# The sums of layer two's weight blocks as single steps, each tied behind VectorE's newest eviction or maximum

## The chip, the cores and the metric

The kernel runs on one core of a Trainium2 chip. The metric is the device time in microseconds (us) of one execution. Three runs of the kernel before gave 817.4, 818.07 and 819.8 us; their median is 818.07 us. TensorE multiplies matrices into PSUM, VectorE and ScalarE work elementwise and read PSUM, GpSimd works elementwise in SBUF, and SyncE issues the transfers.

## The reference, cut to what matters

Attention whose keys are masked by a hash bucket, then two feed-forward layers. Layer one squares a rectified product; layer two (`moe2`) has a leaky activation.

```python
mask = q_bucket[:, :, :, None] == k_bucket[:, :, None, :]
scores = np.where(mask, scale * np.matmul(q, k.transpose(0, 1, 3, 2)), -1000000000.0)
attn = np.exp(scores - np.max(scores, axis=-1, keepdims=True))
attn = attn / (np.sum(attn, axis=-1, keepdims=True) + 1e-09)
x = heads_side_by_side(np.matmul(attn, v))        # 1536 tokens x 512
h = np.maximum(x @ w_in, 0.0)                      # 512 x 2048
x = h * h @ w_out                                  # 2048 x 512
h = x @ w_in2
out = (np.maximum(h, 0.0) + alpha * np.minimum(h, 0.0)) @ w_out2
```

The host hands the layers' weights over as the bits of float64; the kernel turns them into float32 itself.

## The kernel before, in words

The tokens are cut into four chunks of 384. Attention for chunk 0 comes first. Then layer one runs chunk by chunk (`feed_forward`, 16 steps over the hidden blocks `f`), and while chunks 0 to 2 go through it, the attention of chunks 1 to 3 is issued in between (`following`), in steps that `beside` calls five times per hidden block. A second list of steps, `conversion`, is issued in the same way from the start of chunk 1 to progress 2.9 (chunk 2 nearly done). Layer two comes after all that; its input products use sums of weight blocks (a scheme with seven products for eight), so its weights must be ready in DRAM by then, as float32 and with the sums.

One step of attention of concern here: `scores` multiplies on TensorE (L386), VectorE takes the negated maximum of 128x768 scores (L391, `low`), ScalarE the exponential (L394, `sm`). `p_t` transposes the exponentials on TensorE (L409), and the 128x384 result is copied out of PSUM either by ScalarE (L413) or by VectorE (L415), as a letter in `EVICT` says. These copies are called evictions here. `k_ids` makes a mask (L277) and `hash_bits` a comparison (L241) on VectorE.

The conversion of one weight block (`to_f32`): SyncE loads 512 KB into one of three buffers of the pool `wide` (L603), ScalarE makes the exponent (L613), VectorE masks the sign (L615), shifts the mantissa in (L616) and joins the two (L621); the scratch tiles have one buffer each. For a block of `w_out2` the result goes to DRAM (`ahead`, L628). For `w_in2`, blocks `f` and `f + 8` are a pair (`sums_ahead`): their converted halves a11, a12 and a21, a22 stay in the first half of their `wide` buffers, four sums of 128x256 are written into the second halves by VectorE (L649 to L652), and two stores take the seven parts to DRAM (L654, L655). There are 8 pairs. A pair has eight steps before: load and convert the first block; load and convert the second block, with the four sums and both stores; then load and convert of two blocks of `w_out2`, in turn. All 64 steps are spread evenly over 1.9 chunks.

The order on each engine's queue is the planner's. It goes through the program in the order of issue, and lets an instruction that it takes to be ready go before an earlier one that it takes to be waiting. `tc.add_manual_dep(later, earlier, NoSync)` is an order that the planner must keep; between two instructions of one engine it needs no semaphore. Layer one's own weights are fetched by SyncE (L683, `wf`), split by ScalarE (L665) and VectorE or GpSimd (L666), in the same stretch.

Of the kernel before, what the change touches and what calls it, by code (L numbers as in the profile page):

```python
# [7 lines left out]
F32 = mybir.dt.float32  # L8
# [5 lines left out]
ALU = mybir.AluOpType  # L14
# [15 lines left out]
def kernel(  # L30
# [20 lines left out]
    nc = tc.nc  # L51
# [3 lines left out]
    P = 128  # L55
# [11 lines left out]
    def pool(name, bufs, stack=ctx, **kw):  # L67
        return stack.enter_context(tc.tile_pool(name=name, bufs=bufs, **kw))

    const = pool("const", 1)  # L70
    dram = pool("scr", 1, space=DRAM)
# [10 lines left out]
    state = {"attention": True, "moe": False, "s": 0, "m": 0, "h": 0, "whole": state_whole}  # L82
# [14 lines left out]
    def s_tile():  # L97

        state["s"] += 1
        if not state["moe"] and state["s"] % 2 == 0:  # L100
            return ps_a.tile([P, 3, 512], F32, tag="acc", name="acc")
        return ps_s.tile([P, 2, 512], F32, tag="s", name="s")

    def m_tile():

        state["m"] += 1
        if not state["moe"] and state["m"] % 3 == 0:
            return ps_h.tile([P, 512], F32, tag="h", name="h")
        return ps_m.tile([P, 512], F32, tag="m", name="m")
# [94 lines left out]
    class Pair:  # L204
# [175 lines left out]
        def scores(self, h, t):  # L380
            ps = s_tile()
            qs = slice(t * P, (t + 1) * P)
            for a in range(2):
                ks = slice(a * HALF, (a + 1) * HALF)
                for i in range(2):
                    nc.tensor.matmul(  # L386
                        ps[:, a, 0:HALF], self.q[:, h, i, qs], self.k[:, h, i, ks], start=i == 0, stop=i == 1
                    )

            low = p4.tile([P, 1], F32, tag="low", name="low")  # L390
            low_ins = nc.vector.tensor_reduce(low, ps[:, 0:2, 0:HALF], AX.XY, ALU.max, negate=True)  # L391
            sm = sm3.tile([P, S], F32, tag="sm", name="sm")
            i = h * NTB + t
            sm_ins = nc.scalar.activation(  # L394
                sm.rearrange("p (a n) -> p a n", a=2), ps[:, 0:2, 0:HALF], AF.Exp, bias=low,
                accum_out=self.sums[:, i:i + 1],
            )
            scored[self.c, self.j, i] = (low_ins, sm_ins)
            self.p[h, t] = sm

        def p_t(self, h, t, a):
            if t == 0 and a == 0:
                self.pt[h] = p2.tile([P, NTB, NKB, P], F32, tag="pt", name="pt")
            pp = self.p[h, t]
            ps = m_tile()
            n = NKB // 2
            for i in range(n):
                b = a * n + i
                nc.tensor.transpose(ps[:, i * P:(i + 1) * P], pp[:, b * P:(b + 1) * P], ident)  # L409
            src = ps[:, 0:n * P].rearrange("p (b n) -> p b n", b=n)  # L410
            dst = self.pt[h][:, t, a * n:(a + 1) * n, :]
            if EVICT[self.c][2 * t + a] == "a":
                nc.scalar.activation(dst, src, AF.Copy)  # L413
            else:
                nc.vector.tensor_copy(dst, src)  # L415

        def av(self, part):

# [175 lines left out]
    w_bits = {}  # L594
# [5 lines left out]
    def load_bits(u):  # L600
        l, f, o = u
        t = state["wide"].tile([P, DM, 2], U32, tag="wide", name="wbits")
        nc.sync.dma_start(out=t.rearrange("p n b -> p (n b)"), in_=(WO if o else WI)[l][f].bitcast(U32))  # L603
        w_bits[u] = t

    def to_f32(u, w=None):


        if u not in w_bits:
            load_bits(u)  # L610
        t = w_bits.pop(u)
        e = state["conv"].tile([P, DM], F32, tag="we", name="we")
        nc.scalar.activation(e, t[:, :, 1].bitcast(F32), AF.Copy, scale=2.0 ** -112)  # L613
        s = state["conv"].tile([P, DM], U32, tag="wsg", name="wsg")
        nc.vector.tensor_scalar(s, t[:, :, 1], 0x80000000, None, ALU.bitwise_and)  # L615
        nc.vector.scalar_tensor_tensor(s, t[:, :, 0], 29, s, ALU.logical_shift_right, ALU.bitwise_or)  # L616
        w = e if w is None else w
        eu, su = e.bitcast(U32), s
        if len(w.shape) == 3:
            eu, su = [a.rearrange("p (a n) -> p a n", a=2) for a in (eu, su)]  # L620
        nc.vector.scalar_tensor_tensor(w.bitcast(U32), eu, 3, su, ALU.logical_shift_left, ALU.bitwise_or)  # L621
        return w

    def ahead(u):

        w = to_f32(u)
        w_d[u] = dram.tile([P, DM], F32, tag="w%d_%d_%d" % u, name="w%d_%d_%d" % u)
        nc.sync.dma_start(out=w_d[u], in_=w)  # L628

    NF = KFF // 2  # L630
    HM = DM // 2
    sums_of = {}

    def sums_ahead(f, second):

        u = (1, f + NF * second, 0)
        if u not in w_bits:
            load_bits(u)  # L640
        w = w_bits[u].rearrange("p n b -> p (n b)").bitcast(F32).rearrange("p (a n) -> p a n", n=HM)
        to_f32(u, w[:, 0:2])
        if not second:
            sums_of[f] = w
            return
        v = sums_of.pop(f)
        a11, a12, s1, s2 = [v[:, i] for i in range(4)]
        a21, a22, s3, s4 = [w[:, i] for i in range(4)]
        nc.vector.tensor_tensor(s1, a21, a22, ALU.add)  # L649
        nc.vector.tensor_tensor(s3, a11, a21, ALU.subtract)  # L650
        nc.vector.tensor_tensor(s2, s1, a11, ALU.subtract)
        nc.vector.tensor_tensor(s4, a12, s2, ALU.subtract)  # L652
        w_sum[f] = dram.tile([P, 7, HM], F32, tag=f"ws{f}", name=f"ws{f}")
        nc.sync.dma_start(out=w_sum[f][:, 0:4], in_=v)  # L654
        nc.sync.dma_start(out=w_sum[f][:, 4:7], in_=w[:, 1:4])  # L655

    w_sum = {}
    PLACE = (0, 1, 4, 2, 3, 5, 6)
# [166 lines left out]
    def second_x(c, tile):  # L825

        cell = []

        def begin():
            y = state["xraw"].tile([P, NTB, DM], F32, tag="xraw", name="yb")  # L830
            nc.sync.dma_start(out=y, in_=y_d[c])
            cell.append(y)
            cell.append(new_raw(c))

        def block(t):
            ps = tile()
            for m in range(KDM):
                nc.tensor.transpose(ps[:, m * P:(m + 1) * P], cell[0][:, t, m * P:(m + 1) * P], ident)
            nc.scalar.activation(
                cell[1][:, :, t * P:(t + 1) * P], ps.rearrange("p (m n) -> p m n", m=KDM), AF.Copy  # L840
            )

        return [begin] + [lambda t=t: block(t) for t in range(NTB)]
# [44 lines left out]
    def slot(name, dt=F32R):  # L888
        return state["slots"].tile([P, 2048], dt, tag="slot", name=name)
# [18 lines left out]
    def w_load(f):  # L908
        if f < NF:
            raw_sums[f] = slot("wraw", F32)[:, 0:7 * HM].rearrange("p (a n) -> p a n", n=HM)  # L910
            nc.sync.dma_start(out=raw_sums[f], in_=w_sum[f])

    def w_part(f):
        if f < NF:
            w = raw_sums.pop(f)
            t = [slot("wp")[:, 0:7 * HM].rearrange("p (a n) -> p a n", n=HM) for _ in range(2)]
            for i, j in ((0, 4), (4, 7)):
                nc.scalar.activation(t[0][:, i:j], w[:, i:j], AF.Copy)  # L918
                nc.gpsimd.tensor_tensor(t[1][:, i:j], w[:, i:j], f32(t[0][:, i:j]), ALU.subtract)  # L919
            loaded[f] = t  # L920

    def wide_hidden(n, between):


        xh, xl = x_parts[n]
        half = [state["g"].tile([P, NF, 2, T], F32, tag=f"g{i}", name=f"g{i}") for i in range(2)]
        quarter = {f"{i + 1}{k + 1}": half[i][:, :, k] for i in range(2) for k in range(2)}

        def leaky(q, h, f):

            col = f + NF * (q[0] == "2")
            up = state["sums"].tile([P, T], F32, tag="up", name="up")
# [11 lines left out]

        for f in range(NF):
            w_load(f + 2)
# [79 lines left out]
    for i in range(2):  # L1026
        low_ins, sm_ins = scored[0, 2, 2 * NTB - 1] if i == 0 else scored[0, 3, NTB - 1]
# [7 lines left out]
    steps, ends = attention_beside()  # L1035
    following = Background(steps, [(0.0, 0)] + [(c + LEAD, n) for c, n in enumerate(ends)])
    steps = []
    for f in range(NF):
        for k in range(2):
            u = (1, f + NF * k, 0)  # L1040
            steps += [lambda u=u: load_bits(u), lambda f=f, k=k: sums_ahead(f, k)]
        for u in ((1, f, 1), (1, f + NF, 1)):
            steps += [lambda u=u: load_bits(u), lambda u=u: ahead(u)]

    conversion = Background(steps, [(1.0, 0), (NCH - 1.1, len(steps))])

# [4 lines left out]
    for c in range(NCH - 1):  # L1051
# [18 lines left out]
        reason="needed late only",  # L1070
# [14 lines left out]
    steps = second_x(2, bank) + x_sums(1)  # L1085
# [78 lines left out]
```

## Time and profile before

| | |
|---|---|
| median of 3 runs | 818.07 us (817.4 to 819.8) |
| the profiled execution's own time | 819.41 us |
| its span, first to last instruction | 817.4 us |
| mean granted clock of TensorE, as a share of 2.4 GHz | 0.995 |
| busy, share of the span | TensorE 95%, VectorE 67%, ScalarE 62%, GpSimd 38% |
| conversion of layer two's weights and its sums | from about 215 to 470 us |

The profile is one execution. Its times count from the first instruction. "PE" is TensorE's matmul, "PEld" its weight load, "DVE" VectorE, "ACT" ScalarE, "POOL" GpSimd, "SP" SyncE. An instruction is named by its line in the kernel (L415) and by what it writes and reads (`pt<-m`). Idle time of an engine that does not set the pace costs nothing.

### The profile page before, as it was taken

The page shows a single profiled execution, that of the slowest core. Times are in us where ns is not written, and L with a number is a line of the kernel's source. Part 1 is how long each engine was busy: PE and PEld are TensorE (multiplying, and loading weights), DVE is VectorE, ACT ScalarE, POOL GpSimd, SP SyncE. Part 2 cuts the span into 40 slices and gives each one's busy share as a digit, 9 for nine tenths or more (in the row PEclk, how much of TensorE's full clock was granted, in tenths as well). Part 3 has the DMA queues.
Part 4 walks back from the last instruction along what each step waited for, and adds up shares of the span by engine and source line. Part 5 has one row for each costly group of instructions (what it writes and reads, how often), then busy time and mean ns, then how long its engine had stood idle before and what let it go on. Part 6 is the DMA issues. An engine that isn't in the chain of part 4 may idle for free.

```text
span 817.4 us, 12516 instructions
## 1 busy us (share of the span) xinstructions
PE 776.8 (95%) x4330; PEld 634.9 (78%) x4330; DVE 545.8 (67%) x876; ACT 505.8 (62%) x988; POOL 313.3 (38%) x231
## 2 busy tenths in 40 slices
PE   6999899999999999999999998999999999999998
PEld 3665777776768767677776878999998888999886
DVE  8678899887757667788977956754665732665111
ACT  5778778766656556565665648764765525776331
POOL 1012323232356645643342355001563446663440
PEclk9999999999999999999999999999999999999999
DMA  6857878778678787677677568530311226421222
GB/s 181 212 159 229 259 228 269 241 218 243 174 223 265 225 226 242 210 242 264 203 237 232 174 218 286 171 130 1 135 27 52 65 95 221 141 68 44 65 65 90
DMA packets 56707, 143.66 MB, mean 176 GB/s; under 512 B 7402, under 2 KB 11652, under 8 KB 56644
## 3 DMA queue, kind: packets, MB, share of 16 engines
q1 hardware_dynamic: 56644, 142.87, 55.6%
q8 instruction: 34, 0.56, 0.3%
q14 instruction: 29, 0.24, 0.1%
HBM read 96.62 MB, written 25.47 MB: 149 GB/s over the span
## 4 chain that ended last, share of the span: by engine, by line
PE 44%; DVE 4%; DMA 3%; ACT 3%; issue 2%; POOL 1%; SPq 0%; ACTq 0%; POOLq 0%; DVEq 0%
PE b L1000 5%; PE b L1001 5%; PE b L1006 5%; PE b L896 4%; PE b L898 4%; PE b L897 4%; PE m L425 2%; PE h L704 1%; PE s L386 1%; PE h L705 1%; PE h L706 1%; PE acc L749 1%; PE m L409 1%; PE acc L728 1%; PE acc L735 1%
## 5 line engine op out<-in xcount | busy, mean ns | idle before, releaser
L666 POOL TENSOR_TENSOR wl<-wf,wh 128x512 fp32r<-128x512 f32 x64 | 89.0, 1393 | 82.1 <-ACT wh L665 76.4
L665 ACT ACTIVATE wh<-wf 128x512 fp32r<-128x512 f32 x128 | 79.5, 628 | 49.4 <-PE h L705 24.0
L919 POOL TENSOR_TENSOR wp<-wraw,wp 128x1024 fp32r<-128x1024 f32 (+1 forms) x32 | 68.4, 2161 | 99.8 <-ACT wp L918 92.1
L394 ACT ACTIVATE sm<-s,low 128x768 f32<-128x768 f32 x84 | 75.6, 901 | 45.9 <-DVE low L391 45.6
L717 POOL TENSOR_TENSOR gl<-g,gh 128x384 fp32r<-128x384 f32 x48 | 53.1, 1106 | 131.4 <-ACT g L714 64.9
L391 DVE TENSOR_REDUCE low<-s 128x1 f32<-128x768 f32 x84 | 80.0, 953 | 32.9 <-PE s L386 32.4
L990 POOL TENSOR_TENSOR gp<-g,gp 128x768 fp32r<-128x768 f32 x32 | 60.6, 1894 | 81.6 <-ACT gp L989 81.4
L386 PE MATMUL s<-k,q 128*128 128x384 f32 x336 | 80.0, 357 | 10.8 <-ACT sm L394 9.7
L409 PE MATMUL m<-ident,sm 128*128 128x128 f32 x531 | 85.4, 277 | 4.9 <-DVE pt L415 2.4
L409 PEld LDWEIGHTS m<-ident,sm 128*128 128x128 f32 x531 | 65.4, 141 | 22.7 <-DVE pt L415 3.4
L704 PE MATMUL h<-xh,wh 128*128 128x384 f32 x212 | 77.9, 367 | 2.1 <-DVE u L472 1.7
L386 PEld LDWEIGHTS s<-k,q 128*128 128x128 f32 x336 | 58.1, 192 | 26.9 <-ACT sm L394 16.8
L896 PE MATMUL b<-xph,wp 128*128 128x384 f32 x224 | 75.3, 343 | 3.4 <-DVE b L942 1.9
L1000 PE MATMUL b<-wp,gp 128*128 128x512 f32 x192 | 75.1, 391 | 0.0
L898 PE MATMUL b<-xph,wp 128*128 128x384 f32 x224 | 75.0, 335 | 0.0
L897 PE MATMUL b<-xpl,wp 128*128 128x384 f32 x224 | 75.0, 335 | 0.0
L1001 PE MATMUL b<-wp,gp 128*128 128x512 f32 x192 | 74.8, 389 | 0.0
L706 PE MATMUL h<-xh,wl 128*128 128x384 f32 x212 | 72.3, 341 | 0.3 <-POOL wl L666 0.3
L705 PE MATMUL h<-xl,wh 128*128 128x384 f32 x212 | 72.3, 341 | 0.0
L986 DVE TENSOR_TENSOR wp<-wp 128x512 fp32r<-128x512 f32 x28 | 23.1, 830 | 67.6 <-ACT wp L985 67.5
L425 PE MATMUL m<-pt,vr 128*64 128x384 f32 x336 | 66.2, 498 | 0.6 <-ACT pt L413 0.6
L666 DVE TENSOR_TENSOR wl<-wf,wh 128x512 fp32r<-128x512 f32 x64 | 50.9, 804 | 21.3 <-ACT wh L665 20.8
(180 smaller groups left out, 1829.8 us busy)
## 6 DMA issues: line engine op xcount, KB each, us to landing
wf<-w SPq DMA_DIRECT2D x96, 256.0 KB, 3.2
wbits<-in_w_in_dram SPq DMA_DIRECT2D x32, 512.0 KB, 4.6
wbits<-in_w_out_dram SPq DMA_DIRECT2D x32, 512.0 KB, 4.2
wraw<-ws SPq DMA_DIRECT2D x16, 896.0 KB, 4.7
q<-q SPq DMA_DIRECT2D x48, 192.0 KB, 3.2
w<-wf SPq DMA_DIRECT2D x32, 256.0 KB, 2.2
wp<-w SPq DMA_DIRECT2D x32, 256.0 KB, 2.5
k<-kh SPq DMA_DIRECT2D x14, 384.0 KB, 5.5
```

Source lines behind the costliest of these rows:

```text
L386: nc.tensor.matmul(ps[:, a, 0:HALF], self.q[:, h, i, qs], self.k[:, h, i, ks], start=i == 0, stop=i == 1)
L409: nc.tensor.transpose(ps[:, i * P:(i + 1) * P], pp[:, b * P:(b + 1) * P], ident)
L425: nc.tensor.matmul(self.o[r, 0:T], self.vr[:, b, r], self.pt[h][:, :, b, :], start=(b == 0), stop=(b == NKB - 1),)
L666: engine.tensor_tensor(lo, w, f32(hi), ALU.subtract)
L704: nc.tensor.matmul(hp, wih[:, ks], xh[:, kk, :], start=first, stop=False)
L705: nc.tensor.matmul(hp, wih[:, ks], xl[:, kk, :], start=False, stop=False)
L706: nc.tensor.matmul(hp, wil[:, ks], xh[:, kk, :], start=False, stop=last)
L896: nc.tensor.matmul(ps, w[0][:, ms], gh, start=first, stop=False, skip_group_check=True)
L897: nc.tensor.matmul(ps, w[0][:, ms], gl, start=False, stop=False, skip_group_check=True)
L898: nc.tensor.matmul(ps, w[1][:, ms], gh, start=False, stop=last, skip_group_check=True)
L1000: nc.tensor.matmul(a, g[:, 0, b], w[:, 0], start=f == 0, stop=False)
L1001: nc.tensor.matmul(a, g[:, 0, b], w[:, 1], start=False, stop=False)
```

## The change

Three things. First, `state["paced"]` always holds the newest maximum (L391) or VectorE eviction (L415) that was issued. Second, `sums_ahead` hands out six steps for a pair: convert the first block, convert the second, and the four sums one by one, each tied behind `state["paced"]` on VectorE; the first store goes out with the second sum, the other with the fourth. Third, a pair has twelve steps, of which the order is: the two conversions; the load of the first `w_out2` block with the first sum; the second, third and fourth sum; conversion of that block; load of the second `w_out2` block; an empty step; both loads of the next pair; conversion of the second `w_out2` block; an empty step. With two steps ahead of the first pair these are 98 steps, over the same 1.9 chunks.

```diff
             low_ins = nc.vector.tensor_reduce(low, ps[:, 0:2, 0:HALF], AX.XY, ALU.max, negate=True)
+            state["paced"] = low_ins
...
-                nc.vector.tensor_copy(dst, src)
+                state["paced"] = nc.vector.tensor_copy(dst, src)
...
+    def behind(later, earlier):
+        tc.add_manual_dep(
+            later.ins, earlier.ins.name,
+            mybir.DependencyInfo(mybir.DependencyClass.NoSync, mybir.DependencyReason.DATA),
+            reason="the order on their engine",
+        )
+    def paced(ins):
+        behind(ins, state["paced"])
...
-        nc.vector.tensor_tensor(s1, a21, a22, ALU.add)
-        nc.vector.tensor_tensor(s3, a11, a21, ALU.subtract)
-        nc.vector.tensor_tensor(s2, s1, a11, ALU.subtract)
-        nc.vector.tensor_tensor(s4, a12, s2, ALU.subtract)
-        w_sum[f] = dram.tile([P, 7, HM], F32, tag=f"ws{f}", name=f"ws{f}")
-        nc.sync.dma_start(out=w_sum[f][:, 0:4], in_=v)
-        nc.sync.dma_start(out=w_sum[f][:, 4:7], in_=w[:, 1:4])
+    def sums_ahead(f):
+        def convert(second):
+            u = (1, f + NF * second, 0)
+            w = w_bits[u].rearrange("p n b -> p (n b)").bitcast(F32).rearrange("p (a n) -> p a n", n=HM)
+            to_f32(u, w[:, 0:2])
+            sums_of[f, second] = w
+        def first():
+            v, w = sums_of[f, 0], sums_of[f, 1]
+            paced(nc.vector.tensor_tensor(v[:, 2], w[:, 0], w[:, 1], ALU.add))
+        def second():
+            v = sums_of[f, 0]
+            paced(nc.vector.tensor_tensor(v[:, 3], v[:, 2], v[:, 0], ALU.subtract))
+            w_sum[f] = dram.tile([P, 7, HM], F32, tag=f"ws{f}", name=f"ws{f}")
+            nc.sync.dma_start(out=w_sum[f][:, 0:4], in_=v)
+        def third():
+            v, w = sums_of[f, 0], sums_of[f, 1]
+            paced(nc.vector.tensor_tensor(w[:, 2], v[:, 0], w[:, 0], ALU.subtract))
+        def fourth():
+            v, w = sums_of.pop((f, 0)), sums_of.pop((f, 1))
+            paced(nc.vector.tensor_tensor(w[:, 3], v[:, 1], v[:, 3], ALU.subtract))
+            nc.sync.dma_start(out=w_sum[f][:, 4:7], in_=w[:, 1:4])
+        return lambda: convert(0), lambda: convert(1), first, second, third, fourth
...
+    def rest():
+        pass
+    def loads(f):
+        if f < NF:
+            load_bits((1, f, 0))
+            load_bits((1, f + NF, 0))
+    steps += [lambda: loads(0), rest]
     for f in range(NF):
-        for k in range(2):
-            u = (1, f + NF * k, 0)
-            steps += [lambda u=u: load_bits(u), lambda f=f, k=k: sums_ahead(f, k)]
-        for u in ((1, f, 1), (1, f + NF, 1)):
-            steps += [lambda u=u: load_bits(u), lambda u=u: ahead(u)]
+        s, (a, b) = sums_ahead(f), ((1, f, 1), (1, f + NF, 1))
+        steps += [
+            s[0], s[1], lambda a=a, s=s: (load_bits(a), s[2]()), *s[3:], lambda a=a: ahead(a),
+            lambda b=b: load_bits(b), rest, lambda f=f: loads(f + 1), lambda b=b: ahead(b), rest,
+        ]
```

## Rows read from the trace of the kernel before

**Rows 1.** Windows, 215 to 480 us; columns as in its heading row, us busy (instructions).

```profile
core 0: us, PE busy (x) PEld busy (x) DVE busy (x) ACT busy (x) POOL busy (x), PEclk, DMA share, GB/s
215.00:480.00 265.00, 253.28 (x1445) 194.74 (x1444) 201.20 (x322) 157.70 (x319) 122.65 (x105) 0.99 0.71 225
```

**Rows 2.** Timeline, TensorE: start us, us, instruction, [idle before, what ended it].

```profile
219.60 0.62 PE L386 MATMUL s<-k,q 128*128 128x384 f32 x2 [1.07 <-DVE kr L277]
...
289.59 0.33 PE L253 MATMUL m<-bits,code 128*128 128x96 bf16 x4 [1.32 <-DVE pt L415]
...
317.32 0.68 PE L409 MATMUL m<-ident,sm 128*128 128x128 f32 x3 [1.99 <-DVE pt L415]
...
332.48 0.55 PE L409 MATMUL m<-ident,sm 128*128 128x128 f32 x3 [0.60 <-DVE bits L241]
...
353.88 0.79 PE L386 MATMUL s<-k,q 128*128 128x384 f32 x3 [1.85 <-ACT sm L394]
...
393.83 0.80 PE L386 MATMUL s<-k,q 128*128 128x384 f32 x3 [1.05 <-ACT sm L394]
...
462.54 0.80 PE L386 MATMUL s<-k,q 128*128 128x384 f32 x3 [1.48 <-ACT sm L394]
```

**Rows 3.** Waits of TensorE, 215 to 480 us: total us, times, longest.

```profile
PE m L441 <- DVE pt L415: 1.6, 2, 1.0
...
PE h L706 <- POOL wl L666: 0.3, 1, 0.3
```

**Rows 4.** Timeline, VectorE, ahead of the wait that ends at 317.32 us.

```profile
312.99 1.42 DVE L649 TENSOR_TENSOR wbits<-wbits 128x256 f32<-128x256 f32 x1
...
315.75 1.04 DVE L651 TENSOR_TENSOR wbits<-wbits 128x256 f32<-128x256 f32 x1
316.72 0.55 DVE L415 COPY pt<-m 128x384 f32<-128x384 f32 x1
```

**Rows 5.** Timeline, GpSimd, at the same place.

```profile
312.83 2.72 POOL L666 TENSOR_TENSOR wl<-wf,wh 128x512 fp32r<-128x512 f32 x2 [3.62 <-ACT wh L665]
```

**Rows 6.** Windows at TensorE's clock changes; the third number from the end is the clock.

```profile
317.70:320.90 3.20, 3.20 (x11) 2.71 (x10) 2.03 (x4) 2.22 (x5) 0.02 (x1) 0.50 1.03 344
321.00:324.00 3.00, 3.00 (x21) 2.77 (x20) 2.15 (x4) 1.62 (x4) 2.14 (x2) 1.00 0.99 341
...
355.20:358.50 3.30, 3.30 (x12) 2.95 (x11) 1.66 (x3) 2.09 (x4) 1.46 (x2) 0.50 0.95 325
```

**Rows 7.** Timeline, VectorE, a pair's last sum ahead of the wait ending at 353.88 us.

```profile
348.27 1.52 DVE L652 TENSOR_TENSOR wbits<-wbits 128x256 f32<-128x256 f32 x1
```

**Rows 8.** Timeline, VectorE, a sum ahead of the wait ending at 462.54 us.

```profile
458.07 1.51 DVE L649 TENSOR_TENSOR wbits<-wbits 128x256 f32<-128x256 f32 x1
```

**Rows 9.** Lines, VectorE, 215 to 470 us: count, busy us, mean ns, idle before.

```profile
L391 DVE TENSOR_REDUCE low<-s 128x1 f32<-128x768 f32 x44 | 41.9, 953 | 21.1 <-PE s L386 20.9
L415 DVE COPY pt<-m 128x384 f32<-128x384 f32 x61 | 33.1, 550 | 14.8 <-PE m L409 14.7
L616 DVE SCALAR_TENSOR_TENSOR wsg<-wbits,wsg 128x512 uint32<-128x512 uint32 x31 | 24.9, 804 | 0.7
L615 DVE TENSOR_SCALAR wsg<-wbits 128x512 uint32<-128x512 uint32 x31 | 16.4, 531 | 3.9 <-DMA wbits<-in_w_out_dram 1.9 <-DMA wbits<-in_w_in_dram 1.8
L621 DVE SCALAR_TENSOR_TENSOR wbits<-we,wsg 128x512 uint32<-128x512 uint32 x16 | 13.5, 845 | 2.2 <-ACT we L613 1.8
L621 DVE SCALAR_TENSOR_TENSOR we<-we,wsg 128x512 uint32<-128x512 uint32 x15 | 13.4, 894 | 0.6
...
L652 DVE TENSOR_TENSOR wbits<-wbits 128x256 f32<-128x256 f32 x8 | 6.7, 831 | 0.0
L649 DVE TENSOR_TENSOR wbits<-wbits 128x256 f32<-128x256 f32 x8 | 6.3, 785 | 0.1
L650 DVE TENSOR_TENSOR wbits<-wbits 128x256 f32<-128x256 f32 x8 | 5.9, 737 | 0.0
...
L651 DVE TENSOR_TENSOR wbits<-wbits 128x256 f32<-128x256 f32 x8 | 4.3, 537 | 0.0
```

**Rows 10.** The line that copies out a chunk's result, two per chunk: durations, first and last start.

```profile
L811 DVE COPY y<-acc x6: 677/686/692, 229.9 to 491.4; 128x512 f32<-128x512 f32 x6
```

More of the change, by code (lines that the diff above doesn't have):

```diff
@@ L632 @@
     sums_of = {}
[L634 to L648, printed above, removed]
-        nc.vector.tensor_tensor(s1, a21, a22, ALU.add)
-        nc.vector.tensor_tensor(s3, a11, a21, ALU.subtract)
-        nc.vector.tensor_tensor(s2, s1, a11, ALU.subtract)
-        nc.vector.tensor_tensor(s4, a12, s2, ALU.subtract)
-        w_sum[f] = dram.tile([P, 7, HM], F32, tag=f"ws{f}", name=f"ws{f}")
-        nc.sync.dma_start(out=w_sum[f][:, 0:4], in_=v)
-        nc.sync.dma_start(out=w_sum[f][:, 4:7], in_=w[:, 1:4])
+    def sums_ahead(f):
[20 more added lines that the diff above has]
+        return lambda: convert(0), lambda: convert(1), first, second, third, fourth
     w_sum = {}
```

## The prediction

> **What bounds the kernel now.** I read three views in this order: the busy time of each engine in the stretch that the change can touch, the places in that stretch where TensorE stands idle, and VectorE's own order just ahead of those places. The conversion of layer two's weights, with the sums in it, runs from about 215 to 470 us. In the window from 215 to 480 us TensorE works 253.28 of 265 us, VectorE 201.20, ScalarE 157.70, GpSimd 122.65 [rows 1]. So TensorE sets the pace, and the only time to win is its 11.7 us of idling, and what its clock loses. The later stages hold no sum and I leave them as they are.
>
> TensorE's idle spots [rows 2, 3] all but end on VectorE: directly on an eviction of a transpose (L415) or a mask (L277, L241), or on an exponential (L394) that waited for its maximum (L391). Only 0.3 us ends on GpSimd, none on a transfer. VectorE is not short of time over the whole stretch (76% busy), but it works its queue in order, and what stands ahead of an eviction is what TensorE waits for.
>
> Two kinds of weight work stand there. The **sums** first. At 312.99 us the first three sums of a pair run one behind the other until 316.79 us, and the eviction that TensorE needs comes at 316.72 us [rows 4]; TensorE waits 1.99 us for it and goes on at 317.32 us [rows 2]. The sums are 1.42 and 1.04 us long there, since GpSimd runs its own subtractions from 312.83 us for 2.72 us [rows 5]. Behind that wait TensorE's granted clock is 0.50 (1.2 GHz) from 317.7 to 320.9 us, and 1.00 (2.4 GHz) again from 321 us [rows 6]. The same follows the wait of 1.85 us that ends at 353.88 us: clock 0.50 from 355.2 to 358.5 us [rows 2, 6]. There, a pair's sums ended at 349.79 us [rows 7], and VectorE worked without a pause from them to the maximum that was waited for. At 462.54 us a wait of 1.48 us ends [rows 2], with a sum of 1.51 us first in a row of three [rows 8]. Two more waits, 1.6 us together [rows 3], at 404 and 437 us, have sums within the 2 to 8 us of unbroken VectorE work ahead of them. The other kind are the **conversions** (L615, L616, L621): the waits that end at 219.60, 289.59, 332.48 and 393.83 us, of 1.07, 1.32, 0.60 and 1.05 us [rows 2], have no sum near; 4.0 us in all.
>
> **The change, part by part.** No arithmetic is added or taken away: 8 pairs have 4 sums each before and after, 23.2 us of VectorE (6.7, 6.3, 5.9 and 4.3), and 31 conversions take 68.2 us of it (24.9, 16.4, 13.5 and 13.4) [rows 9]. A tie within one engine's queue adds no wait. What is moved:
>
> The steps. 64 steps were spread over 1.9 chunks, now 98 are. Chunk 0 ends near 229.9 us and chunk 2 near 491.4 us by the copies of its result [rows 10], so a chunk takes 130.5 us, a step 3.9 us before and 2.5 us now; a pair still takes about 31 us. Of twelve steps the conversions have the first two, the seventh and the eleventh; the sums have the third to the sixth.
>
> *The sums, each behind an eviction or maximum.* In the lines view there are 61 such copies and 44 maxima in 255 us [rows 9] (a few copies more stay untied because ScalarE makes them), one in 2.4 us, so each sum finds about one of its own to stand behind. Right after an eviction TensorE has just been served, so one sum of 0.4 to 1.5 us is the most that the next one finds ahead of it, in place of 3.8 us. I therefore take back the 1.99 us wholly, 0.9 of 1.85 (conversions stand in that queue too), 1.0 of 1.48, and 0.9 of the 1.6: 4.8 us, between 0 and the 6.9 us that they sum to. The clock: at 0.50, 11 matmuls were recorded in 3.20 us, at 1.00, 21 in 3.00 us [rows 6], so a low stretch loses 3.2 x (1 - 3.44 / 7.0) = 1.6 us. The first low stretch goes with its wait; of the second, whose wait is halved, I count half: 2.4 us, between 0 and 3.2. **Gross 7.2 us.**
>
> *What single sums still cost.* 93 conversion instructions brought 4.0 us of waits, 0.043 us each; a sum of about their length in a place of its own at the same price costs 32 x 0.043 = 1.4 us, between 0 (always hidden) and 4.8 us (nothing is won by parting them).
>
> *Conversions moved closer.* The eleventh step and the first two of the next pair put three conversions into four steps, 10 us. Three take 6.6 us, and VectorE's other work is (201.2 - 68.2 - 23.2) / 265 = 41%, 4.2 us: 10.8 us of work for 10 us. Before, the worst place was a conversion with its sums: 2.2 + 2.9 + 3.2 = 8.3 us for 7.8 us. So that peak is as high as the old one, but without the sums. I put it at half of the present conversion waits, 2.0 us, between 0 and 8.6 us (the slow rival below).
>
> *Loads and stores.* Both loads of the next pair are issued in one step, three steps (7.5 us) ahead of their use, where it was one step (3.9 us); the first store goes after the second sum in place of the third; the first buffer of a pair is held until the fourth sum, two steps ahead of the load that needs one. All go through SyncE's queue, past the fetches of layer one's weights. No wait of TensorE ends on a transfer in this stretch [rows 3], so I cost them at nothing; the cover is that slack of 5 to 7.5 us. If it is gone, the fetches queue behind a load that waits for its buffer, then the splits, then TensorE.
>
> Sum: 4.8 + 2.4 - 1.4 - 2.0 = 3.8 us less. The profiled execution took 819.41 us (span 817.4), 1.3 us above the median of the three runs, 818.07 us; 819.41 - 3.8 = 815.6 us in its terms, and 818.07 - 3.8 = **814.3 us** as a median.
>
> One rule speaks against parting the sums. The rows show sums of 1.42 and 1.51 us beside GpSimd's work where the typical one takes 0.4 [rows 4, 5, 8]. The Trainium skill, "SBUF — State Buffer", section "Who interferes with whom", says that a VectorE instruction with both inputs in SBUF and a GpSimd instruction that reads SBUF exclude each other, and that whichever comes second is blocked until the first has finished. The lengthened sums agree with it.
>
> **The rivals.** *One sum, one collision.* Sums that run one behind the other share a wait for GpSimd; parted ones can each meet one. GpSimd is busy 46% of the stretch [rows 1]. If every one took 1.5 us [rows 8], VectorE would work 32 x 1.5 = 48 us on them, 25 more; at the conversions' 4.0 us of waits for 68.2 us of work that is 1.5 us, and the time is **815.8 us**. Against it: less than half of them should meet GpSimd. That is the rule above, worked out in this kernel.
>
> *The waits only move.* VectorE's queue holds the conversions whatever is done with the sums, and they have three times the work. If the evictions merely find conversions ahead of them, only the first wait and its low clock go (2.0 + 1.6), against the costs of 3.4: **817.9 us**. The case in which the ties do not part the sums, because no newer eviction was issued between two steps, ends at the same place: a tie keeps a sum from going earlier, but does not keep the next one away. For it: the untied conversions alone bring 4.0 us of waits today. Against: three of the five sum waits have sums directly or nearly directly ahead of the awaited instruction.
>
> *Conversions pile up between pairs (slower).* In the four steps where three conversions meet, VectorE is 0.8 us over, and any lengthened instruction adds 1 us. If each of the seven joints between pairs costs a wait of the present mean of a conversion wait, 1.0 us, and one of them lowers the clock, 7.0 + 1.6 = 8.6 us, the gain of 7.2 less 1.4 for the single sums is outrun: 818.07 - 5.8 + 8.6 = **820.9 us**. It decides once a joint costs over 0.8 us. For it: 10.8 us of work in 10. Against: nothing holds the conversions to their step, and a hole of VectorE earlier may take one in.
>
> **How the numbers follow.** A measurement of this kernel tells a change of about 0.3% (2.5 us) from none, so faster is below 815.6 us, slower above 820.5 us. Chances: the forecast 0.46, collisions 0.09, waits that move 0.25, conversions that pile up 0.20. Faster 0.46, same 0.34, slower 0.20. All gains with no cost would be 10.1 us, 808.0 us; nothing won and the pile-up in full is over 826 us. Those ends need every term on one side; leaving out about 1 in 10 below and above, the range is 810.3 to 821.0 us.
>
> **What would show it.** Right: in the trace after, sums singly behind L415 or L391; TensorE's idle time in 215 to 480 us near 8 to 9 us in place of 11.7; one low stretch of the clock or none there; no wait of TensorE on sums over 1 us. Wrong: waits of TensorE of 1 us or more where L615, L616 and L621 of two or three conversions stand ahead of an eviction, one to each pair; new stretches at clock 0.50; SyncE's fetches of layer one's weights waiting behind a load, with TensorE waiting for a split weight. If the waits are gone and the time is not, another engine has taken over, and I have nothing in the trace that says which.

## The result, and the profile after

The changed kernel is slower: a median of 824.89 us (822.0 to 826.89, 6 runs) against 818.14 us of the kernel before (817.13 to 820.55, 6 runs, same chip); ratio 1.0065, 95% interval 1.0042 to 1.0087. (The ratio is taken from the runs and is not the quotient of the two medians; here and below the two differ by up to 0.2%, so the last digit of a ratio should not be leaned on.) The forecast was 814.3 us, the range ended at 821.0 us.

The profiled execution's span is 823.5 us, 6.1 more than before. Where they arose is read from the copies of the chunks' results (L811 before [rows 10], L831 after). This is the line's row of after: durations, first and last start.

```profile
L831 DVE COPY y<-acc x6: 673/686/693, 231.2 to 496.9; 128x512 f32<-128x512 f32 x6
```

The first copy is 1.2 us late; in the runs below that start the list at the same place it comes between 229.1 and 231.7 us, so this is no more than scatter. From the first copy of chunk 0 to that of chunk 1 it is 137.8 us before and 141.5 us after; from there to chunk 2's, 122.4 and 123.0 us; the rest differs by 0.6 us. So 3.7 us were lost while chunk 1 ran.

Windows of after, 215 to 480 us and the stretch of low clock (columns as in rows 1):

```profile
215.00:480.00 265.00, 248.29 (x1414) 190.70 (x1413) 203.57 (x318) 154.36 (x312) 124.83 (x104) 0.99 0.71 222
...
289.40:296.10 6.70, 5.95 (x27) 5.12 (x27) 3.16 (x7) 2.12 (x5) 2.29 (x2) 0.50 0.76 192
```

TensorE idles 16.7 us there, where it was 11.7 [rows 1]. The two stretches of 3.4 us at clock 0.50 [rows 6] are gone; in their place is one of 6.8 us. TensorE's timeline of after shows the waits of 0.8 us or more in that stretch; the smaller ones and the unchanged one at 220 us are left out:

```profile
252.14 0.49 PE L253 MATMUL s<-bits,code 128*128 128x192 bf16 x4 [1.03 <-ACT sm L395]
...
290.15 0.80 PE L253 MATMUL s<-bits,code 128*128 128x192 bf16 x4 [2.79 <-ACT sm L395]
...
331.07 0.96 PE L386 MATMUL s<-k,q 128*128 128x384 f32 x4 [1.35 <-ACT sm L395]
358.39 0.97 PE L386 MATMUL s<-k,q 128*128 128x384 f32 x4 [0.93 <-ACT sm L395]
368.36 0.97 PE L386 MATMUL s<-k,q 128*128 128x384 f32 x4 [1.63 <-ACT sm L395]
400.00 0.97 PE L386 MATMUL s<-k,q 128*128 128x384 f32 x4 [1.19 <-ACT sm L395]
433.50 0.97 PE L386 MATMUL s<-k,q 128*128 128x384 f32 x4 [1.60 <-ACT sm L395]
446.11 0.27 PE L442 MATMUL m<-ident,rin 128*6 128x128 f32 x1 [1.03 <-DVE pt L416]
470.72 0.97 PE L386 MATMUL s<-k,q 128*128 128x384 f32 x4 [0.86 <-ACT sm L395]
```

Since after runs later, a wait is matched to one of rows 2 by the number of maxima that VectorE has done by then (96 up to 500 us, in every kernel here). By that count the wait of 1.99 us at 317.32 us is gone, as hoped, and so are those at 289.59 and 332.48 us. The wait of 1.85 us at 353.88 us is halved: it is the 0.93 us at 358.39 us. That of 1.48 us at 462.54 us is the 0.86 us at 470.72 us, and that of 1.05 us at 393.83 us the 1.19 us at 400.00 us. Others have come, the longest at 290.15 us; the clock falls to 0.50 while it lasts. VectorE's groups, answering rows 9 (L616, L617 and L622 are the conversion; L658 to L672 the sums):

```profile
L617 DVE SCALAR_TENSOR_TENSOR wsg<-wbits,wsg 128x512 uint32<-128x512 uint32 x31 | 26.3, 847 | 0.6
L616 DVE TENSOR_SCALAR wsg<-wbits 128x512 uint32<-128x512 uint32 x31 | 18.8, 607 | 8.5 <-DMA wbits<-in_w_out_dram 6.8 <-DMA wbits<-in_w_in_dram 1.5
L622 DVE SCALAR_TENSOR_TENSOR we<-we,wsg 128x512 uint32<-128x512 uint32 x16 | 18.5, 1154 | 1.4 <-ACT we L614 0.7
L622 DVE SCALAR_TENSOR_TENSOR wbits<-we,wsg 128x512 uint32<-128x512 uint32 x16 | 14.6, 911 | 4.2 <-ACT we L614 4.1
L672 DVE TENSOR_TENSOR wbits<-wbits 128x256 f32<-128x256 f32 x8 | 6.2, 776 | 0.0
L658 DVE TENSOR_TENSOR wbits<-wbits 128x256 f32<-128x256 f32 x8 | 5.7, 708 | 0.1
L662 DVE TENSOR_TENSOR wbits<-wbits 128x256 f32<-128x256 f32 x8 | 5.2, 653 | 0.0
L668 DVE TENSOR_TENSOR wbits<-wbits 128x256 f32<-128x256 f32 x8 | 4.6, 572 | 0.0
```

The sums did not get longer (21.7 us, 23.2 before). The conversions did: 78.2 us for 68.2, of which one instruction more is 0.9; over all 96 of them it is 79.3 for 70.7 us. That is not the price of the change: with the sums left out of it (below), the fastest kernel of all, they take 78.1 us.

### The profile page after: what moved, and what is told of

Read it like the earlier page. It is cut to its first block, busy times and chain, and to the rows that moved or that the text cites. A ratio compares the mean times of both kernels' runs of the same rounds, so it can differ in the third digit from the quotient of the medians.

```text
span 823.5 us, 12527 instructions
## 1 busy us (share of the span) xinstructions
PE 779.2 (95%) x4330; PEld 635.7 (77%) x4330; DVE 546.5 (66%) x876; ACT 505.4 (61%) x988; POOL 317.2 (39%) x231
## 5 line engine op out<-in xcount | busy, mean ns | idle before, releaser
L686 POOL TENSOR_TENSOR wl<-wf,wh 128x512 fp32r<-128x512 f32 x64 | 91.5, 1431 | 83.9 <-ACT wh L685 77.7
L391 DVE TENSOR_REDUCE low<-s 128x1 f32<-128x768 f32 x84 | 80.0, 952 | 31.7 <-PE s L386 31.2
L410 PEld LDWEIGHTS m<-ident,sm 128*128 128x128 f32 x531 | 65.7, 142 | 21.7 <-DVE pt L416 3.3
L1006 DVE TENSOR_TENSOR wp<-wp 128x512 fp32r<-128x512 f32 x28 | 21.0, 751 | 72.1 <-ACT wp L1005 72.1
```

Source lines behind the costliest of these rows:

```text
L686: engine.tensor_tensor(lo, w, f32(hi), ALU.subtract)
```

## The experiments

The runs were made on three chips, each beside the kernel before on the same chip. Its median there was 819.53 us for the four runs below the change in the table, 817.81 for the next two and for late loads and the kernel before shifted later, and 818.24 for the other four; so kernels are compared by their ratios to it and not by their medians. Chunk 1 is the time from chunk 0's first copy to chunk 1's, idle is TensorE's in 215 to 480 us; both come from one profiled execution of each kernel.

| kernel | median us | ratio, 95% interval | chunk 1, us | idle, us |
|---|---|---|---|---|
| before | 818.14 | 1 | 137.8 | 11.7 |
| after | 824.89 | 1.0065 (1.0042 to 1.0087) | 141.5 | 16.7 |
| steps, no ties | 813.84 | 0.9946 (0.9922 to 0.9970) | 130.6 | 8.8 |
| ties, old steps | 823.95 | 1.0074 (1.0043 to 1.0105) | 141.8 | 15.8 |
| after, no sums | 811.81 | 0.9914 (0.9882 to 0.9946) | 130.4 | 10.2 |
| before, no sums | 817.53 | 0.9975 (0.9955 to 0.9995) | 134.9 | 11.5 |
| ties from pair 2 on | 815.53 | 0.9971 (0.9950 to 0.9991) | 133.0 | 11.2 |
| ties on pairs 0 and 1 | 820.63 | 1.0031 (1.0011 to 1.0051) | 139.2 | 14.1 |
| no ties, late loads | 826.18 | 1.0103 (1.0075 to 1.0132) | 140.3 | 17.1 |
| before, shifted later | 825.12 | 1.0085 (1.0063 to 1.0108) | 139.5 | 16.9 |
| before, shifted earlier | 818.97 | 1.0005 (0.9986 to 1.0024) | 135.4 | 14.3 |
| no ties, shifted later | 822.00 | 1.0045 (1.0018 to 1.0072) | 143.0 | 12.5 |
| after, shifted later | 827.90 | 1.0119 (1.0088 to 1.0149) | 145.7 | 18.1 |
| ties behind the sixth newest | 813.36 | 0.9945 (0.9922 to 0.9968) | 132.0 | 9.1 |

**The two halves of the change.** The steps alone:

```diff
     def paced(ins):
-        behind(ins, state["paced"])
+        return ins
```

> The changed kernel without the ties: the twelve steps of a pair and the single sums stay, but a sum may go wherever the planner puts it. Theory A (the twelve steps put conversions close together, and conversions ahead of maxima and evictions cost the time): as slow as the changed kernel, 823 to 827 us, with conversions that take 75 us or more of VectorE. Theory B (the ties cost: a sum stands in front of the next maximum or eviction): back at 817 to 820 us.

Measured 813.84 us, a ratio of 0.9946 where the change has 1.0065: 1.2%, some 10 us, faster than the change, and below the range of either theory. Theory A falls; the ties cost. The other half, each of the four sums tied but left in one step with the second conversion:

```diff
+        paced(nc.vector.tensor_tensor(s1, a21, a22, ALU.add))
-        nc.vector.tensor_tensor(s1, a21, a22, ALU.add)
...
```

> The kernel before with only the ties: eight steps a pair, the four sums still in one step with the second conversion, each tied behind the newest maximum or eviction. Theory A (steps): 815 to 820 us, TensorE's idle time in the stretch 9 to 13 us. Theory B (ties): 822 to 827 us.

Measured 823.95 us, in theory B's range. The steps bring 0.54%, the ties take 0.74% with the old steps and 1.2% with the new ones.

**What the sums cost at all.** In these two kernels the 32 sums are left out, and the stores send copies of the converted halves (this cut is from the changed kernel):

```diff
-            paced(nc.vector.tensor_tensor(v[:, 2], w[:, 0], w[:, 1], ALU.add))
...
-            nc.sync.dma_start(out=w_sum[f][:, 0:4], in_=v)
+            nc.sync.dma_start(
+                out=w_sum[f][:, 0:4].rearrange("p (r a) n -> p r a n", r=2),
+                in_=v[:, 0:2].unsqueeze(1).to_broadcast([P, 2, 2, HM]),
+            )
```

> The changed kernel with the 32 sums left out (the stores send copies of the converted halves, same bytes). Theory A (conversions in the new steps): it stays slow, 820 us or more, since the sums were not what cost. Theory B (sums in their new places): falls to 813 to 817 us.

> The kernel before with the 32 sums left out in the same way. If the sums cost what the prediction took for them (4.8 us of waits and 2.4 us of clock, 5.8 at the most that could be won net of single sums): 811 to 814 us. If conversions fill their place whatever is done with the sums (waits only move): 816 to 819 us.

The first came out at 811.81 us, a little below theory B's range, the second at 817.53 us, in the range of "waits only move". From the kernel before, all sums together are worth 0.25%, 2.0 us (0.4 to 3.7). From the change, taking out the sums and their ties is worth 1.5%, 12 us, of which the ties are 1.2%; without ties the sums are worth 0.3% in the new steps too (0.9946 against 0.9914), which the intervals do not tell from 0.25%. And in the kernel before, taking the sums away does not take the waiting away: TensorE idles 11.5 us for 11.7. The three long waits that had sums ahead (317.32, 353.88 and 462.54 us) are gone, counted by maxima, but new ones stand elsewhere. The longest is one of 2.50 us behind conversions at 358.88 us, two maxima after the old place, and the clock is 0.50 behind it too, from 359.2 to 362.6 us (TensorE's timeline, then VectorE's, of the kernel before without sums):

```profile
358.88 1.47 PE L386 MATMUL s<-k,q 128*128 128x384 f32 x4 [2.50 <-ACT sm L394]
...
354.34 1.18 DVE L616 SCALAR_TENSOR_TENSOR wsg<-wbits,wsg 128x512 uint32<-128x512 uint32 x1
355.61 1.33 DVE L621 SCALAR_TENSOR_TENSOR we<-we,wsg 128x512 uint32<-128x512 uint32 x1
356.86 0.94 DVE L391 TENSOR_REDUCE low<-s 128x1 f32<-128x768 f32 x1
```

**Where the ties cost.** Up to 223 us VectorE's queue is the same in the steps without ties and in the change. Then, without ties (VectorE's timeline):

```profile
223.61 0.56 DVE L416 COPY pt<-m 128x384 f32<-128x384 f32 x1 [0.17 <-PE m L410]
224.09 0.41 DVE L658 TENSOR_TENSOR wbits<-wbits 128x256 f32<-128x256 f32 x1
224.42 0.42 DVE L668 TENSOR_TENSOR wbits<-wbits 128x256 f32<-128x256 f32 x1
224.75 0.42 DVE L662 TENSOR_TENSOR wbits<-wbits 128x256 f32<-128x256 f32 x1
225.21 0.42 DVE L672 TENSOR_TENSOR wbits<-wbits 128x256 f32<-128x256 f32 x1
226.08 0.96 DVE L391 TENSOR_REDUCE low<-s 128x1 f32<-128x768 f32 x1 [0.45 <-PE s L386]
```

and in the change:

```profile
223.05 0.56 DVE L416 COPY pt<-m 128x384 f32<-128x384 f32 x1 [0.16 <-PE m L410]
225.51 0.96 DVE L391 TENSOR_REDUCE low<-s 128x1 f32<-128x768 f32 x1 [1.91 <-PE s L386]
...
241.93 0.56 DVE L416 COPY pt<-m 128x384 f32<-128x384 f32 x1 [5.34 <-PE m L410]
...
247.46 1.32 DVE L622 SCALAR_TENSOR_TENSOR we<-we,wsg 128x512 uint32<-128x512 uint32 x1
248.69 0.55 DVE L416 COPY pt<-m 128x384 f32<-128x384 f32 x1
249.16 1.04 DVE L658 TENSOR_TENSOR wbits<-wbits 128x256 f32<-128x256 f32 x1
250.12 0.95 DVE L391 TENSOR_REDUCE low<-s 128x1 f32<-128x768 f32 x1
```

The four sums of pair 0, with 0.4 us each, stood in a hole of 1.9 us in which VectorE waits for TensorE anyway. In the change that hole and one of 5.34 us stay empty, and the first sum stands at 249.16 us, behind a conversion and ahead of the maximum on which the wait at 252.14 us ends. In pair 1 more comes together. Ahead of the wait of 2.79 us VectorE works on these, without a pause:

```profile
281.11 0.91 DVE L622 SCALAR_TENSOR_TENSOR wbits<-we,wsg 128x512 uint32<-128x512 uint32 x1
282.05 1.41 DVE L658 TENSOR_TENSOR wbits<-wbits 128x256 f32<-128x256 f32 x1
283.38 0.42 DVE L616 TENSOR_SCALAR wsg<-wbits 128x512 uint32<-128x512 uint32 x1
283.72 0.41 DVE L662 TENSOR_TENSOR wbits<-wbits 128x256 f32<-128x256 f32 x1
284.05 1.31 DVE L617 SCALAR_TENSOR_TENSOR wsg<-wbits,wsg 128x512 uint32<-128x512 uint32 x1
285.29 0.55 DVE L416 COPY pt<-m 128x384 f32<-128x384 f32 x1
285.75 0.75 DVE L668 TENSOR_TENSOR wbits<-wbits 128x256 f32<-128x256 f32 x1
286.42 1.77 DVE L622 SCALAR_TENSOR_TENSOR we<-we,wsg 128x512 uint32<-128x512 uint32 x1
288.12 0.94 DVE L391 TENSOR_REDUCE low<-s 128x1 f32<-128x768 f32 x1
```

The pair's second block is joined only at 281.11 us (274.85 us without ties); why so late was not traced. The first sum follows it at once, so its tie held nothing there. The other three come between evictions and maxima, and the conversion of the next block, which nothing holds, goes in between them; without ties it begins behind all four. No run ties pair 0 alone, so what is pair 1's own doing and what it inherits from pair 0 is not parted. This became theory C: a tie costs by the earlier, empty place that it forbids. It was tested by place and by size:

```diff
     def paced(ins, f):
-        behind(ins, state["paced"])
+        if f >= 2:
+            behind(ins, state["paced"])
...
```

> The changed kernel with the ties of the first two pairs taken off; pairs 2 to 7 keep theirs. Theory C (a tie keeps a sum out of an idle hole of VectorE that lies before its place in the program, and puts it among the conversions that come later; this happens to pairs 0 and 1, whose sums can go up to 25 us earlier): 813 to 818 us, chunk 1 near 131 to 133 us. Rival D (each tied sum costs its share, wherever it is): a quarter of the way back, 820 to 823 us.

The same with `f < 2`:

> The steps of the changed kernel, with ties on the first two pairs only. Theory C: 820 to 825 us, chunk 1 near 139 to 141 us, with the low clock near 290 us back. Rival D: 815 to 818 us.

Both came out as theory C has it. Two of the eight pairs carry most of the price: against the steps without ties, ties on pairs 0 and 1 cost 0.85%, on the six others 0.25%, on all 1.2%. Windows of 222 to 300 us show it: ties on pairs 0 and 1, then ties from pair 2 on, then none (one row of each kernel):

```profile
222.00:300.00 78.00, 72.81 (x416) 56.20 (x415) 50.64 (x74) 42.51 (x86) 40.83 (x35) 0.96 0.75 220
```

```profile
222.00:300.00 78.00, 77.17 (x466) 59.03 (x464) 50.18 (x83) 47.03 (x95) 44.70 (x39) 1.00 0.83 237
```

```profile
222.00:300.00 78.00, 77.83 (x471) 59.98 (x470) 50.41 (x84) 47.64 (x96) 44.27 (x39) 1.00 0.83 247
```

TensorE idles 5.2 us with the first ties (72.81 in the change too, to the digit), and loses about 3 us more, as it works some 6 us at clock 0.50; with ties from pair 2 on it idles 0.8 us, without any 0.2 us. That is about 8 of the ties' 10 us. VectorE is as busy in each (50.2 to 50.8 us), but with the first ties it gets through 74 instructions in that time, otherwise 83 or 84. With the old steps less of the price lies there: TensorE idles 3.5 us in this window with ties, 1.7 us before, and its clock stays at 1.00.

The later waits are mostly not the ties'. Of those in the change, the ones at 331.07, 368.36, 400.00 and 433.50 us stand at the same maxima in the steps without ties (1.19, 0.72, 1.01 and 1.81 us) and in the change without sums (1.02, 0.72, 1.01 and 1.55 us): they come with the new steps, and conversions stand right ahead of their maxima. Those at 358.39 and 470.72 us come with the ties of pairs 2 to 7, where they are 0.95 and 0.89 us, and in neither of those two kernels.

Then the size of a tie's hold; here `state["paced"]` is a list to which each maximum and VectorE eviction is appended:

```diff
     def paced(ins):
-        behind(ins, state["paced"])
+        behind(ins, state["paced"][-6])
```

> The changed kernel, with each sum tied behind the sixth newest eviction or maximum in place of the newest, so that it may go five of them earlier. Theory C (the tie costs by how much earlier work it forbids): most of the ties' price is gone, 813 to 818 us, chunk 1 near 131 to 134 us. If a tie costs by itself: 822 to 827 us.

813.36 us: the price is gone. A tie costs nothing in itself (0.9945 against 0.9946 without ties), and leave to go five evictions or maxima earlier was enough here. Pair 0's second sum goes out right ahead of the long hole (VectorE's timeline):

```profile
235.02 0.41 DVE L662 TENSOR_TENSOR wbits<-wbits 128x256 f32<-128x256 f32 x1
240.42 0.56 DVE L416 COPY pt<-m 128x384 f32<-128x384 f32 x1 [4.98 <-PE m L410]
...
242.28 1.37 DVE L672 TENSOR_TENSOR wbits<-wbits 128x256 f32<-128x256 f32 x1
...
244.44 1.15 DVE L616 TENSOR_SCALAR wsg<-wbits 128x512 uint32<-128x512 uint32 x1
```

The hole itself stays all but empty here too (4.98 us), and the hole of 1.9 us is empty as in the change. What differs from the change is that all four sums are done before the next block's conversion begins, the last with 1.37 us. So the place that counts seems to be the one ahead of the conversions, and not the hole as such; no run parts the two further.

**Is it only chance of places?** The list of conversion steps, moved by 0.02 of a chunk for no purpose: later in three of the kernels, as here, and in the kernel before also earlier (0.98 and 1.12):

```diff
-conversion = Background(steps, [(1.0, 0), (NCH - 1.1, len(steps))])
+conversion = Background(steps, [(1.02, 0), (NCH - 1.08, len(steps))])
```

> The kernel before with its list of conversion steps begun and ended 0.02 of a chunk (2.6 us) later, for no purpose. If the time hangs on where single instructions happen to fall in VectorE's queue, it moves by 2.5 us or more either way; if it hangs on the arrangement of steps and ties, 817 to 822 us.

> The kernel before with its list of conversion steps begun and ended 0.02 of a chunk earlier, the other way from the earlier shift. Rival E: anywhere from 813 to 826 us, 2.5 us or more from 818. If 818 us is what the arrangement is worth and the later shift met a mishap: 816 to 820 us.

> The steps without ties, with the list of steps begun and ended 0.02 of a chunk later, as was done with the kernel before (which it took from 818 to 825 us). If the twelve steps are worth 5 to 6 us whatever falls where: 813 to 817 us. If their gain is a lucky place of some instructions (rival E): 818 us or more.

> The changed kernel with the same shift of 0.02 of a chunk. Theory C (the ties hold the first pairs' sums out of idle holes): slower than the run without ties and with the same shift, by 4 us or more. Rival E (chance of places): no order between the two, either sign.

Later by 2.6 us costs the kernel before 0.85%, the steps without ties 0.99%, the change 0.54%; earlier changes nothing. So a purposeless move of the list is as large as the whole effect, and the size of each effect holds for its place only. The ties' sign held: with the shift, too, they cost (1.0119 against 1.0045, 5.9 us), as theory C expected. The steps' sign held in the time (1.0045 against 1.0085), but the two intervals overlap, and chunk 1 has it the other way round (143.0 against 139.5 us): the shifted kernel before loses its time ahead of that, its first copy starting at 234.49 us, 229.94 us before. There a conversion at the head of VectorE's queue waits 2.95 us for its load at 225.88 us. The expectation that the steps' gain would come out at 813 to 817 us was wrong; 822.00 us is what rival E, a lucky place, expected.

One thing that the shift does is seen in the shifted steps without ties (VectorE's timeline, then TensorE's): the conversion at the head of VectorE's queue waits 4.32 us for its load, and the eviction behind it, and with it TensorE, waits too.

```profile
258.79 0.43 DVE L616 TENSOR_SCALAR wsg<-wbits 128x512 uint32<-128x512 uint32 x1 [4.32 <-DMA wbits<-in_w_out_dram]
259.13 0.55 DVE L416 COPY pt<-m 128x384 f32<-128x384 f32 x1
...
259.74 0.90 PE L410 MATMUL m<-ident,sm 128*128 128x128 f32 x3 [2.27 <-DVE pt L416]
```

Last, the loads. The steps without ties, each load one step ahead of its conversion (a pair's second block two):

```diff
-            s[0], s[1], lambda a=a, s=s: (load_bits(a), s[2]()), *s[3:], lambda a=a: ahead(a),
-            lambda b=b: load_bits(b), rest, lambda f=f: loads(f + 1), lambda b=b: ahead(b), rest,
+            s[0], s[1], s[2], *s[3:5], lambda a=a, s=s: (s[5](), load_bits(a)), lambda a=a: ahead(a),
+            rest, rest, lambda b=b: load_bits(b), lambda b=b: ahead(b), lambda f=f: loads(f + 1),
```

> The steps without ties, but each load one step (2.5 us) ahead of its conversion where the change has it three or four steps ahead. If the gain of the steps (819.5 to 813.8 us) comes from the early loads: 817 us or more, with more idle time of VectorE that ends on a load. If it comes from the conversions and sums being steps of their own: 812 to 816 us.

826.18 us by time speaks for the early loads. But VectorE's idle time on the converted blocks' loads is only 6.1 us there and 4.4 us with early loads, and the longest waits (2.56 and 3.17 us) have sums beside GpSimd's work ahead of them. Nor does such idle time order the kernels: it is 8.3 us in the change, but 7.8 us with ties from pair 2 on, and 3.7 us before. With a shift worth 0.85 to 0.99% beside it, what made the steps faster stays open.

## Why the prediction was wrong, point by point

*The bound* was right: TensorE sets the pace, its waits end on VectorE's order, and the clock falls with the long ones (1.99 and 1.85 us before, 2.79 us after).

*The ties* are the step that failed. The prediction put them at nothing ("A tie within one engine's queue adds no wait") and said that each sum "finds about one of its own to stand behind" and that "one sum of 0.4 to 1.5 us is the most that the next one finds ahead of it". It looked at what stands behind an eviction and did not ask where the sum would stand without the tie. The trace of before had the answer (VectorE's timeline):

```profile
222.29 0.41 DVE L649 TENSOR_TENSOR wbits<-wbits 128x256 f32<-128x256 f32 x1
...
223.41 0.42 DVE L652 TENSOR_TENSOR wbits<-wbits 128x256 f32<-128x256 f32 x1
```

The sums of pair 0 ran from 222.29 to 223.83 us, while chunk 1, with whose fourth step they are issued, began only near 229.9 us [rows 10]. The planner had put them into idle time ahead of their place in the program. A tie only keeps an instruction from going earlier, which the prediction says itself under its second rival; what it forbade was worth 0.74% with the old steps and 1.2% with the new, 6 to 10 us, where the sum has nothing.

*The gross gain* was taken back in part. By the count of maxima, the change wins 1.99, 0.92 and 0.62 us of the three long waits with sums ahead, 3.5 us where 3.9 were forecast, and both low stretches of the clock. But a wait that goes is not yet time won: with all sums out of the kernel before, the three are gone as well, the idle time is nearly the same (11.5 us), and the gain is 2.0 us, where parting them was put at 7.2 gross. The rival "the waits only move" had this right, for the kernel before.

*Conversions moved closer* were put at 2.0 us, and the slow rival had them as its cause. Its waits did come: 331.07, 368.36 and 433.50 us, 4.6 us together, have conversions right ahead, and they come without ties and without sums too. They do not make the kernel slow, for the steps alone, with 3.7 us of waits at the same places, are 0.54% faster than before. What made it slow are the waits ahead of 300 us and the low clock there; with the list at this place the new steps have them only with ties on the first pairs. So the rival's time, 820.9 us, nearer to the result than the forecast, came from another cause. Its counter-argument, that nothing holds a conversion to its step, is seen in pair 1: the next block's conversion goes ahead, in between the sums.

*The rest of the sum* can be held against the steps without ties: 813.84 us and 8.8 us of idle time, where 814.3 us and 8 to 9 us were forecast. How much of that is luck shows in the shift, which takes the same kernel to 822.00 us.

*One sum, one collision* was not seen: the sums took 21.7 us, less than before. What got longer is the conversions. The Trainium skill, "SBUF — State Buffer", section "Who interferes with whom", states that a VectorE instruction with two inputs in SBUF contends with a GpSimd instruction that reads SBUF, and a conversion's join is such an instruction as well as a sum. This trace agrees: the join at 286.42 us takes 1.77 us beside GpSimd's split, 0.69 us elsewhere (277 us). GpSimd's timeline:

```profile
286.18 1.47 POOL L686 TENSOR_TENSOR wl<-wf,wh 128x512 fp32r<-128x512 f32 x1
```

*Loads and stores* at nothing: in the change no wait of TensorE is put down to a transfer. But in the shifted kernel a load held VectorE and TensorE through the queue, a way that "No wait of TensorE ends on a transfer in this stretch" does not exclude.

*The range* took in only rivals in which the ties did no harm, and so ended below the result.

## What to carry to other kernels

Before tying filler work behind something, read in the trace where the planner puts it now, against its place in the program: if it goes there ahead of that place, a tight tie forbids it, and here that cost 0.74 to 1.2%; a loose tie (here the sixth newest) cost nothing at the one place tried. To price filler work, take it out and look at the whole time: here its waits went, and others of nearly the same sum came. And shift such a list by a little before a difference of less than 1% is put down to its arrangement; the version with new steps and no ties, 813.84 us, and that with loose ties, 813.36 us, beat both kernels at this place of the list only.

## What the runs showed that was not expected

Moving the start of a list of background steps by 2.6 us of some 820 changed the time by 0.54 to 0.99% in three arrangements, always for the worse, and the same move the other way, tried in one, by nothing that can be measured. And one long wait of TensorE cost about as much again in clock: after 2.79 us of waiting that end at 290.15 us, TensorE worked 5.95 us at 0.50 until 296.1 us, of which half, 3.0 us, is lost by estimate, where shorter waits, up to 1.63 us, in the same profile left the clock at 1.00.
